# Attention and spectral mixing on one core: how three weight tiles are cut into transfers

## The chip, the core and the metric

The kernel runs on one core of one Trainium2 chip. Its time is the device time of one execution in microseconds (us). The core has five engines that matter here: PE (TensorE, matrix products; its weight loads are listed as PEld), DVE (VectorE), ACT (ScalarE), POOL (GpSimd) and SP (SyncE). Besides these it has 16 DMA engines that move data between the chip's main memory and the core's on-chip memory. To keep the two kinds apart, this text calls a DMA engine a **lane**.

## The reference, cut to what matters

```
attention over 8 batches, 8 heads, 576 positions, 64 per head:
  heads 0-3 see the last 32 positions, heads 4-7 every 32nd position before them
x = attention output as (8, 576, 512)
X = rfft(x, axis=1)[:, :64]                       # 64 modes, real part Xr, imaginary part Xi
Yr = Xr @ w_r - Xi @ w_i                          # one 512x512 matrix of each kind per mode
Yi = Xr @ w_i + Xi @ w_r
u = x + irfft(Y)                                  # Y is zero beyond the 64 modes
out = u + relu(u @ w_ch)
```

The two weight arrays moe_w_r and moe_w_i have shape (64, 512, 512) in 32-bit floats, 64 MB each. Every element is used once per execution, for all 8 batches.

## The kernel before, in words

The program works in stages. First come the four strided heads of the 8 batches, then the four local heads, with the Fourier transform of each finished batch into 64 modes (`dft`). Beside the local heads and after them, PE multiplies the spectra by the weights mode by mode (`mode`, `mode_pair`, L585 to L647). Then w_ch is applied, the spectra are brought back to positions, and the output is written at the end, by SP.

**Weights.** The input dimension is cut into two halves of 256 rows. A weight tile `wt` (L164 and L166) holds one half of two neighbouring modes, in 16-bit floats: 128 partitions of 2 modes x 4 x 512 elements. Partitions 0 to 63 hold the real part, from moe_w_r, and partitions 64 to 127 the imaginary part, from moe_w_i. One partition, called a **row** below, is 8 KB in the tile (two pieces of 4 KB, one per mode) and 16 KB in main memory, since the transfer also turns 32-bit into 16-bit floats. There are 64 tiles. `w_fetch` (L157) makes one tile's transfers; the list `ORDER` (L150) says which half and modes are next, and the index `i` counts modes, so tiles have even `i`.

**Transfers.** POOL issues all loads of weights and of q, k and v, on one queue. A tile normally takes two transfers of 512 KB: the 64 real rows (L186, moe_w_r) and then the 64 imaginary rows (L186, moe_w_i). The last two tiles, and mode 0's imaginary part, are loaded one mode at a time (L190). The dictionary `UNEVEN` (L152) names three tiles whose real part is cut by rows into pieces, each a transfer of its own (L182): tile i = 64 into 25, 12 and 27 rows, tile 80 into 6, 54 and 4, tile 96 into 10 and 54.

**What sets the order.** Nothing is scheduled automatically: instructions run on each engine in the order of the program text. `w_fetch` is called after the products that use up a tile (L608, L638), because the new tile takes that tile's buffer; there are 5 buffers in the pool, and three more tiles lie in space that is used for something else later (`GUEST`). POOL's transfers use 8 semaphores in turn, so a transfer is issued only after the one eight places before it has landed in full, that is, on all its lanes. PE's products on a tile wait for both of its parts. The last products are those of L630, after which come a short chain through `spec_z` (L741), ACT, and the output loop (L1063 to L1088).

Of the kernel before, what the change touches and what calls it, by code (L numbers as in the profile page):

```python
# [56 lines left out]
def kernel(  # L57
# [91 lines left out]
    SPLIT1, SPLIT0 = 56, 48  # L149
    ORDER = [(1, m) for m in range(SPLIT1)] + [(0, m) for m in range(SPLIT0)]  # L150
    ORDER += [(1, m) for m in range(SPLIT1, NM)] + [(0, m) for m in range(SPLIT0, NM)]
    UNEVEN = {64: (25, 12, 27), 80: (6, 54, 4), 96: (10, 54)}  # L152
    w_tiles = []
    w_chs = {}
    w_ch = big.tile([128, 4, DM], F16, name="w_ch")
# [1 line left out]
    def w_fetch(n=1):  # L157
        for _ in range(n):
# [9 lines left out]
            for ri, src in enumerate((moe_w_r, moe_w_i)):  # L168
# [8 lines left out]
                if ri and not m:  # L177
                    ones = [1]
                elif i in UNEVEN and not ri:
                    a = 0  # L180
                    for n in UNEVEN[i]:
                        nc.gpsimd.dma_start(dst[a : a + n], rows[a : a + n])  # L182
# [937 lines left out]
```

## Time and profile before

| what | us |
|---|---|
| runs | 426.20, 426.51, 426.53 |
| their median | 426.51 |
| the profiled execution | 426.5 |
| its span, first to last instruction | 424.7 |
| PE busy | 341.0 |
| DVE busy | 234.6 |
| ACT busy | 218.9 |
| POOL busy | 110.7 |
| issue of the three tiles' first pieces | 218.32, 256.30, 296.81 |
| landing of the last weight transfer | 391.40 |

The span is that of the instructions; 1.8 us of the execution lie around it. A POOL entry in the trace is the issue of a transfer, some 0.6 us, and not the transfer itself, which lands some 18 us later. The share of the DMA engines in a view is their mean busy share; since a packet of 4 KB is recorded with 324 ns while the next one on its lane starts 304.5 ns after it, a lane that is never idle is shown as 1.06.

### The profile page before, as it was taken

How to read it: one execution, taken by the hardware profiler on the slowest of the kernel's cores; microseconds unless marked ns; L12 is line 12 of the kernel's file. 1: busy time of each engine (PE TensorE's matmuls, PEld its weight loads, DVE VectorE, ACT ScalarE, POOL GpSimd, SP SyncE). 2: the span in 40 equal slices, each digit the busy share in tenths (PEclk: the TensorE clock that was granted, in tenths of full speed). 3: DMA queues.
4: the chain of work that ended last, by engine and by line, in shares of the span. 5: the costliest groups of instructions: out<-in, count | busy, mean ns of one | idle time of the engine just before them, and what ended most of it. 6: DMA issues, size and time to landing. Idle time of an engine off the chain costs nothing.

```text
span 424.7 us, 9761 instructions
## 1 busy us (share of the span) xinstructions
PE 341.0 (80%) x4167; PEld 205.9 (48%) x4167; DVE 234.6 (55%) x466; ACT 218.9 (52%) x391; POOL 110.7 (26%) x196
## 2 busy tenths in 40 slices
PE   2977878769999698889758589778788866988994
PEld 2866766654656365566423344435345422544331
DVE  3788778851455154356113346845676363664785
ACT  1687778643656366656642334423443443543773
POOL 7332333322422222222222322222232221220000
PEclk9999999967999699999995989999999968999998
DMA  8999999999999999999999999999999999996598
GB/s 147 212 213 213 213 211 213 211 212 211 213 215 213 211 215 213 214 213 215 210 214 212 214 212 215 211 213 214 213 213 213 214 213 215 213 213 137 205 357 329
DMA packets 30842, 91.62 MB, mean 216 GB/s; under 512 B 4368, under 2 KB 5136, under 8 KB 30800
## 3 DMA queue, kind: packets, MB, share of 16 engines
q0 software_dynamic: 25168, 81.28, 96.6%
q1 hardware_dynamic: 5200, 9.65, 6.2%
q8 instruction: 32, 0.52, 0.5%
q10 hardware_dynamic: 432, 0.08, 0.1%
q14 instruction: 10, 0.08, 0.0%
HBM read 162.83 MB, written 9.44 MB: 406 GB/s over the span
## 4 chain that ended last, share of the span: by engine, by line
DMA 52%; PE 25%; DVE 12%; ACT 4%; issue 3%; POOL 1%; DVEq 0%; POOLq 0%; ACTq 0%
DMA wt<-in_moe_w_i_dram 36%; DMA wt<-in_moe_w_r_dram 12%; PE y L597 5%; DMA ring<-in_q_dram 3%; DVE xb L241 3%; DVE kz L283 2%; ACT X L251 2%; PE p L993 2%; PE sc L532 1%; PE p L1007 1%; PE tp L413 1%; PE y L532 1%; DVE yy L757 1%; DMA ring<-in_v_dram 1%; PE sc L459 1%
## 5 line engine op out<-in xcount | busy, mean ns | idle before, releaser
L597 PE MATMUL y<-wt,X 128*32 128x512 f16 (+1 forms) x448 | 68.1, 415 | 22.7 <-DMA wt<-in_moe_w_i_dram 22.2
L186 POOL DMA_DIRECT2D wt<-in_moe_w_r_dram x59 | 34.6, 587 | 118.5 <-PE y L597 28.2
L186 POOL DMA_DIRECT2D wt<-in_moe_w_i_dram x60 | 35.4, 589 | 75.3 <-DMA wt<-in_moe_w_i_dram 52.9
L597 PEld LDWEIGHTS <-X 128*32 128x32 f16 (+1 forms) x448 | 27.9, 139 | 40.3 <-DMA wt<-in_moe_w_i_dram 20.2
L731 ACT ACTIVATE v<-sc 128x512 f16<-128x512 f32 x32 | 19.1, 597 | 44.5 <-PE sc L722 44.5
L732 DVE COPY xo<-tp 128x512 f16<-128x512 f16 x32 | 22.1, 691 | 35.4 <-PE tp L730 35.4
L722 PE MATMUL sc<-w_cp,xT 128*128 128x512 f16 x128 | 36.1, 404 | 1.9 <-DVE xT L690 1.9
L241 DVE TENSOR_TENSOR xb<-av,rec 90x256 f16<-90x256 f32 (+2 forms) x80 | 36.0, 450 | 2.8
L489 ACT ACTIVATE PL<-sc 128x480 f16<-128x480 f32 (+1 forms) x48 | 26.9, 578 | 20.3 <-PE sc L475 19.9
L240 DVE RECIPROCAL rec<-av 90x4 f32<-90x4 f32 (+2 forms) x80 | 14.6, 182 | 38.1 <-PE av L504 28.2
L251 ACT ACTIVATE yr<-y 128x512 f16<-128x512 f32 x28 | 16.7, 597 | 35.8 <-PE y L597 35.7
L967 DVE TENSOR_TENSOR xo<-p,xo 128x1024 f16<-128x1024 f32 x16 | 19.6, 1224 | 20.8 <-PE p L765 20.7
L420 DVE COPY qT<-tp 128x576 f16<-128x576 f16 x16 | 11.9, 752 | 34.1 <-PE tp L413 34.1
L251 ACT ACTIVATE v<-p 128x1024 f16<-128x1024 f32 x16 | 16.4, 1024 | 22.4 <-PE p L765 22.4
L378 ACT ACTIVATE PL<-sc 90x360 f16<-90x360 f32 (+1 forms) x48 | 22.7, 490 | 7.1 <-PE sc L371 6.5
L251 ACT ACTIVATE v<-tp 128x640 f16<-128x640 f16 (+1 forms) x24 | 19.0, 806 | 11.5 <-PE tp L447 9.3
L413 PE MATMUL tp<-cI_s,ring 64*64 64x64 f16 x864 | 22.2, 195 | 2.8 <-DVE qT L420 2.4
L459 PE MATMUL sc<-cMl_s,cI_s 128*128 128x480 f16 (+1 forms) x48 | 19.0, 395 | 4.8 <-ACT PL L489 3.2
L276 PE MATMUL tp<-cI_s,ring 72*128 72x72 f16 x256 | 15.4, 207 | 9.1 <-DMA ring<-in_v_dram 7.7
L251 ACT ACTIVATE kz<-tp 64x360 f16<-64x360 f16 (+1 forms) x32 | 18.9, 592 | 6.1 <-PE tp L413 5.1
L413 PEld LDWEIGHTS <-ring 64*64 64x64 f16 x864 | 17.3, 109 | 9.1 <-issue 5.1
L1030 ACT ACTIVATE rl<-p 128x1024 f32<-128x1024 f32 (+1 forms) x19 | 18.4, 979 | 5.7 <-PE p L1007 3.0
(142 smaller groups left out, 734.7 us busy)
## 6 DMA issues: line engine op xcount, KB each, us to landing
wt<-in_moe_w_i_dram POOLq DMA_DIRECT2D x60, 512.0 KB, 18.9
wt<-in_moe_w_r_dram POOLq DMA_DIRECT2D x59, 512.0 KB, 18.0
out_dram<-osb SPq DMA_DIRECT2D x17, 512.0 KB, 3.3
ring<-in_v_dram POOLq DMA_DIRECT2D x8, 288.0 KB, 13.2
ring<-in_q_dram POOLq DMA_DIRECT2D x8, 288.0 KB, 13.4
ring<-in_k_dram POOLq DMA_DIRECT2D x8, 288.0 KB, 13.0
ring<-in_v_dram POOLq DMA_DIRECT2D x3, 512.0 KB, 14.9
ring<-in_q_dram POOLq DMA_DIRECT2D x3, 512.0 KB, 14.8
```

The costliest lines, as they stand in the source:

```text
L186: nc.gpsimd.dma_start(dst, rows)
L241: nc.vector.tensor_tensor(out=dst, in0=val.rearrange("p h (q c) -> p h c q", c=4), in1=rec[0:n, 0:pieces] .to_broadcast((n, pieces, 64)) . ...
L251: nc.scalar.activation(out=out, in_=in_, func=ACTF.Copy)
L378: nc.scalar.activation(out=PS[0:n, ds(POFF[t], 4 * n)], in_=scp[0:n, 0 : 4 * n], func=ACTF.Exp, scale=SCALE,)
L413: nc.tensor.transpose(tp[ds(64 * hp, 64), ds(64 * i, 64)], qn[ds(64 * hp, 64), ds(64 * (9 * g + i), 64)], idn[ds(64 * hp, 64), ds(64 * hp, ...
L459: nc.tensor.matmul(scp[:, 0 : n * times].rearrange("p (h x) -> p h x", h=times), idn, mask_rows("cMl", n, times), start=True, stop=False,)
L489: nc.scalar.activation(out=dst, in_=src, func=ACTF.Exp, scale=SCALE)
L597: nc.tensor.matmul(yp[ds(a, 32), :], Xh[half][pr, c].rearrange("p b r (h m) -> p (b r h) m", h=2)[:, :, mm % 32], wt[pr, XC[c], :], start= ...
L722: nc.tensor.matmul(vp, xT[:, ch], w_chs["cp"][:, ch, :], start=(ch == 0), stop=(ch == 3),)
L731: nc.scalar.activation(out=v0, in_=vp, func=ACTF.Copy)
L732: nc.vector.tensor_copy(out=xo.rearrange("p (h q c) -> p h q c", h=2, c=4), in_=tp[:, 0:512].rearrange("p (h c q) -> p h q c", h=2, c=4),)
L967: nc.vector.tensor_tensor(out=xo, in0=up[:, 0:n], in1=xo, op=AluOp.add)
```

## The change

The dictionary `UNEVEN` keeps one entry with other numbers. The real part of tile 64 comes as 16, 35 and 13 rows, and the real parts of tiles 80 and 96 are each loaded as one transfer of 64 rows by L186, as those of the other tiles are. All else is the same.

```diff
-    UNEVEN = {64: (25, 12, 27), 80: (6, 54, 4), 96: (10, 54)}
+    UNEVEN = {64: (16, 35, 13)}
```

## The prediction

> **What bounds the kernel now.** I read the page's slices first, then the stretches of the span, then the chain of waits.
>
> ```profile
> DMA  8999999999999999999999999999999999996598
> GB/s 147 212 213 213 213 211 213 211 212 211 213 215 213 211 215 213 214 213 215 210 214 212 214 212 215 211 213 214 213 213 213 214 213 215 213 213 137 205 357 329
> q0 software_dynamic: 25168, 81.28, 96.6%
> DMA 52%; PE 25%; DVE 12%; ACT 4%; issue 3%; POOL 1%; DVEq 0%; POOLq 0%; ACTq 0%
> ```
>
> From slice 2 to slice 36 the lanes are full, at 211 to 215 GB/s, and one queue (q0, POOL's loads) does it. How the loads end is in the stretches (the columns are us, POOL busy, granted clock, DMA share, GB/s):
>
> ```profile
> 385.00:386.00 1.00, 0.00 (x0) 1.00 1.01 205
> 386.00:387.00 1.00, 0.00 (x0) 1.00 0.98 193
> 387.00:388.00 1.00, 0.00 (x0) 1.00 0.95 188
> 388.00:389.00 1.00, 0.00 (x0) 1.00 0.79 156
> 389.00:390.00 1.00, 0.00 (x0) 1.00 0.52 102
> 390.00:391.00 1.00, 0.00 (x0) 1.00 0.17 33
> ```
>
> A full lane shows 1.06. The share falls over 6 us, so the 16 lanes finish the same queue at very different times. The lane time missing from 385 on is (0.05 + 0.08 + 0.11 + 0.27 + 0.54 + 0.89)/1.06 = 1.8 us per lane: an even split of the same bytes would end 1.8 us sooner. And the last lane is what the end waits for (chain of waits: start, us, what):
>
> ```profile
> 381.41 9.99 DMA wt<-in_moe_w_i_dram
> 391.40 0.14 issue
> 391.54 0.65 PE y L630 x16
> ```
>
> PE had stood idle 0.52 us there for that transfer. What comes after, up to 424.7, needs those products, so **the end moves one for one with the lane that finishes last**. The change moves rows between lanes; that is its whole price, and I work it out lane by lane.
>
> **Lanes from packets.** The trace keeps start, length and size of every packet. On one lane a 4 KB packet is followed after 304.5 ns, and each transfer ends with a 4-byte receipt that takes 20.7 ns. By these two steps the packets sort into 16 lanes. A whole part puts 4 rows on each (8 packets, 2.46 us). The pieces do not spread like that:
>
> ```profile
> wt<-in_moe_w_r_dram POOLq DMA_DIRECT2D x2, 432.0 KB, 17.0
> ...
> wt<-in_moe_w_r_dram POOLq DMA_DIRECT2D x1, 216.0 KB, 14.4
> wt<-in_moe_w_r_dram POOLq DMA_DIRECT2D x1, 200.0 KB, 16.1
> ```
>
> The 54 rows (432 KB) lie on 9 lanes, 6 rows each; the 27 on 9, 3 each; the 25 on 5, 5 each; 12, 10, 6 and 4 rows on as many lanes, one each. In each case that is the largest divisor of the rows up to 16. A lane without a share gets, for two packets of a row, two 4-byte fillers instead. The count closes: under 512 B the page has 4368 packets, and 213 transfers x 16 receipts + 384 of constants + 576 fillers is 4368. On the first tile one lane has (5, 1, 0) rows of the three pieces, four have (5, 0, 3), five (0, 1, 3), six (0, 1, 0): each piece begins on the lane after the one where the last piece stopped, round a ring of 16. I number the places 0 to 15 from the first lane of the 25 rows. All three tiles fit that ring. In rows over the three real parts (12 is even), with the time of the lane's last receipt:
>
> | places | rows now | last receipt, us |
> |---|---|---|
> | 0 | 13 | 387.0 |
> | 1 to 4 | 15 | 388.3 to 389.9 |
> | 5, 6 | 11 | 390.4, 390.6 |
> | 7, 8 | 16 | 388.9, 389.5 |
> | 9 | 11 | 391.1 |
> | 10 to 12 | 9 | 388.5, 389.9, 390.4 |
> | 13 to 15 | 9 | 385.2, 389.5, 390.7 |
>
> Why lanes differ is seen too: the 32 instruction loads (q8, 16 KB) take 0.9 to 1.15 us each and fall on about half of the lanes; the last, at 385.66, made place 9 the last one.
>
> **The change, part by part.**
>
> *Pieces 16, 35, 13.* By the divisor, 16 rows take 16 lanes, 35 take 7 lanes with 5 rows, 13 take 13 lanes with one. From place 0 that is 7 rows on places 0 to 3, 6 on 4 to 6, 2 on 7 to 15.
>
> *Tiles 80 and 96 whole.* 4 rows on each lane, twice, so 8 more everywhere.
>
> *Sum in rows, new less old:* place 0: 15 - 13 = +2; 1 to 3: 0; 4: -1; 5 and 6: 14 - 11 = **+3**; 7 and 8: -6; 9: -1; 10 to 15: +1. They add to zero. One row is 2 x 304.5 ns = 0.61 us. New ends: places 5 and 6 at 390.4 and 390.6 + 1.83 = 392.2 and 392.4; 13 to 15 at most 390.7 + 0.61 = 391.3; 10 to 12 at most 391.0; 9 at 390.5; all others earlier. Off that comes what is in the lanes besides rows: three receipts fewer (0.06) and, on places 5 and 6, some 20 fillers of 6 to 8 ns (0.14). The last receipt goes from 391.1 to about 392.2: **+1.1 us**.
>
> *Three issues fewer on POOL.* Its order of time around the first tile (start, us, what, idle before):
>
> ```profile
> 218.32 0.70 POOL L182 DMA_DIRECT2D wt<-in_moe_w_r_dram  x1 [2.19 <-DMA wt<-in_moe_w_r_dram]
> 219.17 0.57 POOL L182 DMA_DIRECT2D wt<-in_moe_w_r_dram  x1 [0.16 <-issue]
> 221.63 0.62 POOL L182 DMA_DIRECT2D wt<-in_moe_w_r_dram  x1 [1.88 <-DMA wt<-in_moe_w_r_dram]
> ```
>
> Issues of 0.57 to 0.70 us cost nothing either way: POOL waits about 2 us for a landing before nearly each of them, and a transfer issued 18 us ahead of its landing leaves several in each lane. Were that cover gone, three issues are 2 us. All later transfers take another of the 8 semaphores; each still waits for the one eight before, and this holds more bytes when none of the eight is a piece. No wait is added, and nothing is queued behind one.
>
> *The middle.* Lanes lie up to 9.0 us apart after tile 80 now, and would lie some 7 us apart. Weights would land sooner there, but PE waits only 5.4 us in all for weights from 256 to 313, and the lanes stay full, so nothing of it reaches the end.
>
> *Where the ring begins.* The trace can't show whether an execution starts where the last one stopped. Before's pieces advance it by 64 and its twelve 8-row loads by 96, both multiples of 16, so either way each execution looks alike. The new pieces advance it by 7 + 13 = 20, so it would move on 4 places each time. With the start 4 on, places 4 to 7 take +3 and 8 to 10 +2 against even loads, 9 ends at 392.9: +1.9. Starts 8 and 12 on load the late places 9 to 15: +2.7 and +3.1 by the same sums. I take 1.5, between the profiled start (1.1) and one move (1.9), and keep 1.1 and 3.1 for the range.
>
> **Two rules weighed.** The trace has the 54 rows on 9 lanes and the fillers on 7. The Trainium skill (DMA: Bandwidth & Descriptors, Why a DMA increments its semaphore by 16 and not by 1) states that divisor rule and a round-robin start, but also an exception where such copies go out as rows/16 rounded up per engine; by the exception 35 rows would be 3 on eleven lanes and 2 on a twelfth, and the early lanes alone would be loaded. The trace shows the divisor, not the exception. The same page (Anatomy of one DMA — SWDGE (gpsimd) path) gives each transfer a fixed 2.0 us; as an estimate from it, three fewer would give back 6 us, to about 420. The trace has 0.02 us for a receipt in a full lane, since transfers queue back to back.
>
> **The forecast.** Profiled execution: 424.7 + 1.5 = 426.2 in span, + 1.8 around it = 428.0. Its 426.5 is the median of the runs (426.51), so 428.0 stands for the median too.
>
> **The rivals.**
>
> *No change that can be measured (within 0.2%, about what a measurement here can tell from no change; 425.66 to 427.36).* The instruction loads decide as much as rows: place 5 or 6 took one of 1.05 us at 360.1, the other a smaller one of 0.45 at 343.6. If these fall on other lanes, 5 and 6 end 0.5 to 1 us sooner, the last lane is near 391.3, and the time is 426.7 to 427.2. Against it: they come in the same turn of lanes all through the trace, and the change alters no engine's program but by three issues.
>
> *Faster.* Loading whole ends the crowding of tile 80: its last piece lands 4.2 us after the part before it, where a whole part takes 2.45. If PE, falling behind there, carried that delay to the end, 1.7 us would come back: 424.8. It decides if lanes run dry because buffers come free late. Against it: the share is 1.06 to 1.07 in every stretch from 218 to 382, and there is no lane time to win but the tail. With rows, even the best start can't gain: all whole would end with place 13 to 15 at 390.7 + 1.83 = 392.5.
>
> *Ring moved far (starts 8 and 12):* 429.2 to 429.6, if the start carries over and these executions set the median.
>
> **How the numbers follow.** Slower at the profiled start or one move on, 427.4 to 428.5: 0.54, of which 428.0 is the middle. Moved far: 0.16. Same: 0.20. Faster: 0.10. Range 426.7 to 429.4: it leaves out the faster case and a little at each end. Chances: faster 0.10, same 0.20, slower 0.70.
>
> **What would show it.** The last weight transfer lands near 392.5 to 393.3 instead of 391.40. From 256 to 313 lanes lie nearer together than now, and in the last 6 us further apart, with the share falling for longer. The fillers fall from 384 in the pieces to 9 x 10 + 3 x 2 = 96, and the packets under 512 B from 4368 to 4032 (three times 16 receipts go too); that many says 35 rows lie on 7 lanes and 13 on 13. Runs that differ by steps of about a microsecond would show the ring carried over. A landing at or before 391.40 would prove the sum wrong, a share under 1.0 before 382 the premise.

## The result and the profile after

The changed kernel takes 427.8 us (median of 9 runs, 426.92 to 428.25), the kernel before beside it 426.64 us (9 runs, 426.0 to 427.42). The medians differ by 1.2 us. The ratio is 1.0024, with a 95% interval from 1.0014 to 1.0033, which is a loss of 1.0 us (0.6 to 1.4): small, but clear of no change. A second set of runs (f1 below) gave 428.22 us and 1.0031 [1.0019, 1.0044].

The page of the profiled execution (428.25 us, span 426.5 us):

```profile
DMA packets 30507, 91.62 MB, mean 215 GB/s; under 512 B 4033, under 2 KB 4801, under 8 KB 30465
...
q0 software_dynamic: 24832, 81.28, 96.3%
```

Queue q0 moves the same 81.28 MB in fewer packets. Packets under 512 B are 4033, where the prediction had 4032: q14, a queue of instruction loads, has one packet of 64 bytes more here, and the repeat (f1) has 4032. So the pieces lie as the divisor rule said: 16 rows on 16 lanes, 35 on 7, 13 on 13.

The chain of waits at the end (start, us, what):

```profile
363.52 17.22 DMA wt<-in_moe_w_r_dram
...
383.49 9.60 DMA wt<-in_moe_w_i_dram
393.08 0.14 issue
393.22 0.65 PE y L630 x16
```

It is the chain of before, 1.7 us later: the last weight transfer lands at 393.08 instead of 391.40, and PE starts 0.14 us after it in both. The stretches before that end (us, POOL busy, granted clock of TensorE, DMA share, GB/s):

```profile
386.00:387.00 1.00, 0.00 (x0) 1.00 0.99 197
387.00:388.00 1.00, 0.00 (x0) 1.00 0.88 180
388.00:389.00 1.00, 0.00 (x0) 1.00 0.73 143
389.00:390.00 1.00, 0.00 (x0) 1.00 0.71 139
390.00:391.00 1.00, 0.00 (x0) 1.00 0.40 78
391.00:392.00 1.00, 0.00 (x0) 1.00 0.09 16
392.00:393.00 1.00, 0.00 (x0) 1.00 0.04 8
```

One lane of 16 at 1.06 would show 0.066. From 391.71 on, where the second-latest lane has landed its last packet, the core waits 1.4 us for a single lane, while the other 15 are idle. Traced back by its packets, this lane took five rows of the 35 and one row of the 16 and none of the 13: it is place 5 or 6.

### The profile page after: what moved, and what is told of

It is laid out like the page before. It is cut to its first block, busy times and chain, and to the rows that moved or that the text cites. A ratio compares the mean times of both kernels' runs of the same rounds, so it can differ in the third digit from the quotient of the medians.

```text
span 426.5 us, 9756 instructions
## 1 busy us (share of the span) xinstructions
PE 342.9 (80%) x4167; PEld 206.0 (48%) x4167; DVE 234.8 (55%) x466; ACT 219.1 (51%) x391; POOL 107.9 (25%) x193
## 2 busy tenths in 40 slices
DMA packets 30507, 91.62 MB, mean 215 GB/s; under 512 B 4033, under 2 KB 4801, under 8 KB 30465
## 3 DMA queue, kind: packets, MB, share of 16 engines
q0 software_dynamic: 24832, 81.28, 96.3%
## 4 chain that ended last, share of the span: by engine, by line
DMA 58%; PE 22%; DVE 10%; ACT 4%; issue 3%; POOL 1%; DVEq 0%; POOLq 0%; ACTq 0%
DMA wt<-in_moe_w_i_dram 41%; DMA wt<-in_moe_w_r_dram 12%; DMA ring<-in_q_dram 5%; PE y L597 4%; DVE xb L241 2%; DVE kz L283 2%; ACT X L251 2%; PE p L993 2%; PE sc L532 1%; PE p L1007 1%; PE tp L413 1%; PE sc L459 1%; PE y L532 1%; DVE kz L420 1%; DVE rec L240 1%
## 5 line engine op out<-in xcount | busy, mean ns | idle before, releaser
L597 PE MATMUL y<-wt,X 128*32 128x512 f16 (+1 forms) x448 | 69.1, 421 | 24.1 <-DMA wt<-in_moe_w_i_dram 23.6
L186 POOL DMA_DIRECT2D wt<-in_moe_w_r_dram x61 | 35.5, 582 | 127.8 <-DMA wt<-in_moe_w_r_dram 31.5
L186 POOL DMA_DIRECT2D wt<-in_moe_w_i_dram x60 | 35.0, 583 | 79.7 <-DMA wt<-in_moe_w_i_dram 65.1
```

The costliest lines, as they stand in the source:

```text
L186: nc.gpsimd.dma_start(dst, rows)
L597: nc.tensor.matmul(yp[ds(a, 32), :], Xh[half][pr, c].rearrange("p b r (h m) -> p (b r h) m", h=2)[:, :, mm % 32], wt[pr, XC[c], :], start= ...
```

## The experiments

There are twelve runs. All their kernels differ from the changed one in the dictionary `UNEVEN` at most: f1 is the changed kernel itself, g3 repeats e1, and none leaves out any work. A last landing is always that of the profiled execution. **Theory:** rows decide, lane by lane; the end follows the lane that finishes last, and a piece costs nothing by itself. **Rivals:** pieces cost something as transfers (issues, receipts, semaphores); or the instruction loads decide, by the lane on which they fall.

### All whole (e1, and g3 as its repeat)

```diff
-    UNEVEN = {64: (16, 35, 13)}
+    UNEVEN = {}
```

> All three real parts loaded whole, no pieces at all. Lane theory (the end is the lane that finishes last, at 0.61 us a row): places 10 to 12 get 3 rows more than before and end at 390.4 + 1.83 = 392.2, place 9 one more at 391.7, places 5 and 6 one more at 391.2; the last lane ends 1.1 us later than before, so the time is 1.1 us above before, 0.6 to 1.7 with the instruction loads falling on other lanes. Piece theory (a piece costs time of its own, whole parts save it): at or below the time of before, -0.3 us. Instruction-load theory (only where the 16 KB instruction loads fall matters, rows do not): same as before within 0.5 us.

> All three tiles whole once more, beside the two others. As before: 426.9, at most 0.4 us above the kernel before; between the early pieces (g1) and the changed kernel. Lane theory: last landing 391.6 to 392.1 by which late lane the last instruction loads fall on.

Measured: 426.86 us, ratio to before 1.0005 [0.9996, 1.0014]; the repeat 426.98 us, 1.0006 [0.9997, 1.0015]. So before's eight pieces were worth some 0.2 us (0.6 at most by the intervals), not 1.1, and the expectation of e1 missed. By themselves these two runs would fit the rival of the instruction loads, which had the same time as before within 0.5 us; e3, e4 and f3 below decide against it. The chain of e1:

```profile
382.46 9.63 DMA wt<-in_moe_w_i_dram
392.09 0.14 issue
392.22 0.65 PE y L630 x16
```

The last landing is 0.7 us behind before's in this execution and 1.0 us ahead of the changed kernel's. With even loads the landings also show which lanes are late by themselves. The last transfer lands on its 16 lanes (receipts that the trace records, us) at

```
386.35 386.53 386.85 387.07 387.42 387.59 387.90 388.79
390.45 391.04 391.09 391.42 391.44 391.70 391.82 392.09
```

These are two groups of eight, some 4 us apart in the mean, and between them half of the lanes work, at a share of 8 x 0.066 = 0.53:

```profile
388.00:389.00 1.00, 0.00 (x0) 1.00 0.56 111
389.00:390.00 1.00, 0.00 (x0) 1.00 0.51 102
```

By the prediction's table, less the rows that each place had, places 0 to 4, 7, 8 and 15 are the early lanes, 5, 6 and 9 to 14 the late ones. The instruction loads make the gap. When e1's packets from 256 us on are sorted into lanes, the eight loads of 16 KB lie on the eight late lanes, one on each, and each delays its lane by 1.08 to 1.13 us. Before that end 31 such loads fall on eight lanes, 3.9 on each, which is 4.2 to 4.4 us.

### Half of the change (e2, e3)

```diff
-    UNEVEN = {64: (16, 35, 13)}
+    UNEVEN = {64: (25, 12, 27)}                                        # e2
+    UNEVEN = {64: (16, 35, 13), 80: (6, 54, 4), 96: (10, 54)}          # e3
```

> Half of the change alone: tile 64 keeps 25, 12 and 27 rows, tiles 80 and 96 are whole. Lane theory: places 10 to 15 stay relieved by 3 rows on tile 64 as before, place 9 gets one row more (391.7), places 5 and 6 one more (391.2); last lane 0.6 us later than before, time +0.6 us (0.1 to 1.1). Piece theory: five pieces fewer, between before and below it, 0 to -0.5 us. Instruction-load theory: same within 0.5 us.

> The other half alone: tile 64 in 16, 35 and 13 rows, tiles 80 and 96 in their old pieces. The ring then stands at 4 instead of 10 when tile 80 comes, so the same old pieces lie on other lanes: rows against whole are +2, +7, +7, +2, +2, +2, +2 on places 0 to 6, -2 on 7 to 9, -3 on 10 to 15. Lane theory: places 5 and 6 end at 392.3 to 392.4, places 1 and 2 somewhere from 390.7 to 393.1; time +1.3 us on before (0.9 to 2.0), as slow as the whole change or slower although it has eight pieces as before. Piece theory: as before, within 0.3 us. Instruction-load theory: same within 0.5 us.

Measured: e2 426.82 us, 1.0006 [0.9997, 1.0015]; e3 427.92 us, 1.003 [1.0019, 1.0042]. Loading tiles 80 and 96 whole costs nothing that shows. The numbers 16, 35 and 13 alone bring the whole loss: with five more pieces (three more transfers) e3 is as slow as the changed kernel, though the old pieces of tiles 80 and 96 lie on other lanes there than before.

### The same pieces on other places (e4)

```diff
-    UNEVEN = {64: (16, 35, 13)}
+    UNEVEN = {62: (8, 56), 64: (16, 35, 13)}
```

> The changed kernel with one tile more in pieces: tile 62 comes as 8 and 56 rows, which is nearly even by itself (one row more on places 0 to 5, three fewer on 6 and 7) but moves the ring by 22, so that the 16, 35 and 13 rows of tile 64 begin at place 6 and lie on the late lanes 8 to 12. Lane theory: places 8 and 9 get +3 and 10 to 12 +2 against whole, 9 ends at 393.5 and 10 to 12 at 393.4, 2.3 us later than before; time +2.3 us (1.7 to 2.9), 1.2 us slower than the changed kernel. Piece theory: two pieces more cost a little, +0.1 us on the changed kernel. Instruction-load theory: as the changed kernel within 0.5 us.

Measured: 428.67 us, 1.0051 [1.0038, 1.0064], last landing 393.50. Tile 62's pieces only move the start of the ring by six and are almost even by themselves; with them the late places 9 to 12 get 2 or 3 rows more than even loads have, and some 0.9 us more is lost than by the changed kernel.

### The changed kernel again (f1)

> The changed kernel once more, beside the others. Lane theory, ring starting at place 0 in each execution: places 5 and 6, which are late already, get 2 rows more than in even loads, and the last of them ends near 392.4 to 393.1; 427.2 to 428.3 us, above whole loads by some 1 us. If the start of the ring were carried over from one execution to the next, the profiled one would have an even chance or better of another start: the seven lanes of the 35 rows would not be five early and two late ones, and the runs would lie in steps, up to 429.6. If only the turn of the instruction loads decides, as likely 426.6 as 428.

Measured: 428.22 us (427.61 to 429.07), 1.0031. The profiled execution ends at 392.48, and its pieces show the same start of the ring. The six runs show no steps of a microsecond.

### One set of pieces in two orders (f2, f3)

```diff
-    UNEVEN = {64: (16, 35, 13)}
+    UNEVEN = {64: (15, 25, 24), 80: (25, 24, 15)}      # f2
+    UNEVEN = {64: (24, 25, 15), 80: (24, 25, 15)}      # f3
```

> Lane theory: tiles 64 and 80 in pieces that give places 0 to 4 and 15, the early lanes, 5, 4, 4, 4, 1 and 2 rows more than even loads, and all others, the late ones among them, 2 rows less. The late lanes end 1.2 us sooner than with whole loads, the early ones come up to about 390.0; last landing 390.3 to 391.0, time 425.3 to 426.1, below before by 0.5 to 1.3 us. Rival, that pieces cost in themselves (six pieces here against three in the changed kernel): 428 or above. Rival, that the turn of the instruction loads decides: 426.6 to 427.9.

> The same six sizes in the same two tiles in another order (24, 25, 15 twice). Lane theory: now places 12 to 15 get 4 rows more than even loads, place 0 gets 6, all others 2 less; places 12 to 14 are late lanes and end near 393.7 to 394.5: time 428.8 to 429.7, above before by 2.2 to 3.1 us, and 3 us or more above the other order. Rivals, pieces in themselves or the turn of the instruction loads: the two orders agree within 0.6 us.

Measured: f2 426.85 us, 1.0001 [0.9993, 1.001]; f3 429.63 us, 1.0066 [1.0054, 1.0079]. Six pieces of the same sizes, 2.8 us apart by their order: this is the clearest case against both rivals, that pieces cost something and that the instruction loads decide, for by either the two orders agree. The stretches of f3:

```profile
390.00:391.00 1.00, 0.00 (x0) 1.00 0.21 41
391.00:392.00 1.00, 0.00 (x0) 1.00 0.27 57
392.00:393.00 1.00, 0.00 (x0) 1.00 0.16 33
393.00:394.00 1.00, 0.00 (x0) 1.00 0.10 20
394.00:395.00 1.00, 0.00 (x0) 1.00 0.02 4
```

From 391 on the share is that of three lanes, then two, then one (3 x 0.066 = 0.20, the first stretch with an instruction load at 391.3 besides): the last landings are 392.95, 394.12 and 394.66, by the ring the three late lanes 12 to 14, which got 4 rows more.

f2 missed its number by some 1 us. Its late lanes did land sooner, 390.95 at the latest by the receipts; but one lane of places 0 to 3 landed at 391.70. It carries 4 or 5 rows more than even loads, so by rows it would land at 391.70 - 4 x 0.61 = 389.3 with even loads (388.7 with 5), near the latest of e1's early group (388.79) and not with the rest of it. A load of 8 KB (q14) falls on it at 343.2 and costs it 0.5 us. The estimate had all early lanes alike.

### Fewer rows for all late lanes (f4, g1, g2, h1)

```diff
-    UNEVEN = {64: (16, 35, 13)}
+    UNEVEN = {64: (18, 21, 25), 72: (10, 50, 4), 80: (21, 3, 40), 96: (27, 30, 7)}   # f4
+    UNEVEN = {64: (25, 24, 15)}                                                      # g1
+    UNEVEN = {64: (25, 24, 15), 72: (7, 56, 1), 80: (9, 50, 5), 96: (24, 13, 27)}    # g2
+    UNEVEN = {64: (25, 11, 28), 72: (18, 40, 6), 80: (8, 50, 6), 96: (26, 11, 27)}   # h1
```

> Lane theory: four tiles (64, 72, 80 and 96) in twelve pieces that take 2 to 4 rows from each late lane (places 5, 6 and 9 to 14) and give places 0 to 4 and 15 two to five more, 7 and 8 one: all lanes but 7, 8 and 15 would end between 389.0 and 390.3. Last landing 389.8 to 390.6, time 424.9 to 425.7, below before by 0.9 to 1.7 us. An even split of all lanes, which nothing beats, would be 1.8 us below. Rival, pieces cost in themselves: the slowest of the four. Rival, turn of the instruction loads: 426.6 to 427.9.

> Three pieces on tile 64 only, as in the changed kernel, but 25, 24 and 15 rows: against whole loads place 0 gets 3 rows more, 1 to 4 get 2 more, 5 to 15 one less. Lane theory: the late lanes (5, 6, 9 to 14) end 0.6 us sooner than with whole loads, places 1 to 4 end at 390.0 at most; last landing 390.9 to 391.6, time 426.0 to 426.7, which is 1.5 to 2.2 us below the changed kernel with as many pieces. Rival, three pieces on that tile cost in themselves: like the changed kernel, near 428.2.

> Four tiles in twelve pieces, as in the run with four tiles before, but one lane among places 1 to 3, which that run showed to end 1.4 us later than was taken for it, gets less: places 0 to 4 get 4, 3, 3, 3 and 3 rows more than whole loads, 7, 8 and 15 get 2 more, 5, 6 and 10 to 13 three less, 9 and 14 two less. Lane theory: late lanes end 1.2 to 1.8 us sooner than with whole loads, the lane among 1 to 3 at 390.6; last landing 390.4 to 391.0, time 425.5 to 426.1, below before by 0.5 to 1.2 us. Rival, pieces in themselves, or whatever kept the last run with four tiles at 427.1, keep it there: 427.

> Four tiles in twelve pieces again, without a piece of a single row and with only 2 rows more than whole loads on places 1 to 4, 7, 8 and 15 (place 0 gets 5 more); 5, 6, 9, 10 and 11 get 2 less, 12 to 14 three less. Lane theory, with the one-row piece on two lanes as the cause of 428.7 in the last run with four tiles: late lanes end at 390.8 at the latest, the lane among 1 to 3 at 390.0; last landing 390.4 to 391.1, time 425.5 to 426.3, below before by 0.4 to 1.2 us, the fastest of all. Rival, twelve pieces cost something in themselves or the turn of the instruction loads undoes it: 427 or above.

Measured:

| kernel | last landing | us | ratio to before |
|---|---|---|---|
| f4 | 391.66 | 427.09 | 1.0008 [0.9996, 1.002] |
| g1 | 391.30 | 426.69 | 0.9995 [0.9984, 1.0006] |
| g2 | 393.79 | 428.69 | 1.0037 [1.0023, 1.0051] |
| h1 | 390.58 | 426.24 | 0.9996 [0.9986, 1.0006] |

*f4* missed its 424.9 to 425.7 us as f2 had missed. It again loads places 1 to 3 by 4 rows, and again a single lane is last, 0.7 us behind the next.

*g1* has three pieces on tile 64, like the changed kernel, and ends at 391.30 instead of 393.08 or 392.48. It is what the theory gives for early lanes loaded instead of late ones, and the rival would have put it at 428.2.

*g2* was to be fast and was slow; its count of packets says why, as far as is known:

```profile
DMA packets 30842, 91.62 MB, mean 214 GB/s; under 512 B 4368, under 2 KB 5136, under 8 KB 30800
```

216 transfers of 16 receipts, 384 of constants, 192 fillers of the 8-row loads and 322 of the eleven larger pieces leave 4368 - 4354 = 14 for the piece of one row. If its two packets lay on one lane, 15 lanes would have two fillers each, 30. Fourteen says that the two packets lie on two lanes and 14 lanes have one filler. The ring then moves by 2 and not by 1, and all later pieces lie one place further than planned: place 9, a late one, gets 2 rows more than even loads instead of 2 less, and ends at 393 or later. That the last lane is place 9 is worked out, not seen. By the same count place 0 gets 7 rows more, but it is an early lane, and with 6 more in f3 it is not among the last three as read above. Nor do 2 rows explain all of it: the other kernels with 2 rows more end at 392.5 to 393.1, and g2 ends at 393.79. That part stays open.

*h1*, without such a piece, has the lanes nearest together of all kernels (387.74 to 390.58, against 385.50 to 391.40 before). Its stretches:

```profile
387.00:388.00 1.00, 0.00 (x0) 1.00 0.95 188
388.00:389.00 1.00, 0.00 (x0) 1.00 0.74 148
389.00:390.00 1.00, 0.00 (x0) 1.00 0.34 66
390.00:391.00 1.00, 0.00 (x0) 1.00 0.00 0
```

The profiled execution, 425.69 us, is the shortest of all, and twelve pieces cost nothing that shows. But its runs go from 425.69 to 427.16 us, and against before's the median is only 0.24 us lower, with 1 inside the interval. Of the 0.8 us that its profiled end gains on before's, the runs show at most a part: it can't be said to beat the kernel before.

### What the twelve say together

Rows of the worst late place, counted against even loads (places after the ring), and the end of the profiled execution:

| rows | kernel | last landing |
|---|---|---|
| -2 | h1 | 390.58 |
| -1 | g1; before | 391.30; 391.40 |
| 0 | e1, g3; e2 | 392.09, 391.99; 391.47 |
| +2 | after, f1; e3 | 393.08, 392.48; 392.65 |
| +2 (worked out) | g2 | 393.79 |
| +3 | e4 | 393.50 |
| +4 | f3 | 394.66 |

From -2 to +4 the end moves by 4.08 us, 0.68 a row, where a row is 0.61; kernels of one line differ by up to 0.6 (g2 by more). The runs rise less steeply: by the ratios, from 0.2 us below before (h1) to 2.8 above (f3), 0.5 a row. f2 and f4 (-2) are left out, since an early lane ends last there.

## Why the prediction came out right, step by step

- **The end follows the last lane: shown.** The profiled time less the last landing is 35.10 us before, 35.17 after, and 35.11 to 35.14 in ten of the twelve others, over landings from 390.58 to 394.66. The two exceptions are g2 (35.53) and e2 (35.98). In e2 the transfer landed at 391.47, but the chain is another (g2's is of the same kind):

```profile
390.71 0.64 PE y L630 x16
391.35 0.86 PE p L993 x4
392.21 0.43 PE p L998 x2
392.64 0.49 PE y L630 x16
```

  PE had just begun other products (L993, L998) that stand ahead of the last ones in its program, and finishes them first. So this order is the next bound: the last products begin 1.2 us after the landing in this case, where 0.14 us is the rule.

- **The divisor and the ring: right.** The count of packets and the lanes of the 35 rows agree. The rule gives the count under 512 B of the other kernels too (4224 for f2 and f3, 4416 for h1; g2 by the one-row piece as above), and e4 and f3 use it to put a loss where it is wanted. The exception that the Trainium skill states (DMA: Bandwidth & Descriptors, Why a DMA increments its semaphore by 16 and not by 1), rows over 16 rounded up, would give other fillers and load twelve lanes with the 35 rows, so not the early lanes alone as the prediction has it; 4032 is the divisor's number.

- **Three rows more on places 5 and 6: right lane, right size.** The last receipt was to come at 392.2 to 392.4; it came at 392.73 in the first profiled execution and at 392.13 in f1. The packets of this lane show a load of 16 KB at 277.6 us in the first, with a loss of 1.08 us, and one at 318.5 in f1. That the turn of these loads makes the difference of 0.6 is argued, not shown.

- **The step that was mis-sized: what the old pieces were worth.** The prediction had even loads ending at 392.5 on places 13 to 15, later than the change. e1 and g3 measure 426.86 and 426.98 us, 0.2 to 0.3 us above before by the ratios, and end at 392.09 and 391.99. Two entries of the table were at fault: where two lanes run in step in before's trace, their packets had been read crosswise, and the latest of places 13 to 15 is 389.5 and not 390.7 (the 390.6 or so belongs to one of places 1 to 4). The load of 8 KB at 343.6, which the rival gave to place 5 or 6, lies on that early lane as well. So the loss is not the going of the old pieces; it is the new ones, some 0.8 to 1.1 us (the ratios of the changed kernel and f1 less those of e1 and g3).

- **The ring moved on between executions: not seen.** I took 1.5 us between 1.1 (profiled start) and 1.9 (four places on). The profiled executions of the changed kernel both begin at place 0, and the runs lie in no steps. Without this term the sum of 1.1 stands, and the ratios measure 1.0 and 1.3 us: the lane sum was right, and the 0.4 us added for the ring was not. That 428.0 lies so near 427.8 and 428.2 is in part luck, since the kernel before, too, was 0.1 to 0.3 us slower beside them than the 426.51 the forecast started from. The start in executions without a profile is not shown by any trace.

- **Three issues fewer, nothing: right.** e3, with three transfers more than the changed kernel, is 0.1 us from it, and h1, with twelve pieces and six transfers more, is the lowest of all. The fixed 2.0 us for each transfer that the same page states (Anatomy of one DMA — SWDGE (gpsimd) path) is not to be seen in a queue that stays full.

- **The middle, nothing: right.** Lanes lie 6.9 us apart from 277 on, against up to 9.0 before; PE's waits for weights from 256 to 313 go from 5.4 to 5.0 us, and the end shows nothing of it.

- **The rival "no change", by the instruction loads: part of it stands.** Kernels with the same rows differ by 0.6 us in their profiled ends (393.08 and 392.48), and single runs of one kernel mostly by 1 to 2 us. The turn of the 32 loads begins on different lanes in different profiled executions. That this makes the spread of the runs is argued from the traces; no run varied it alone.

## What to carry to other kernels

Before loads are balanced by hand over DMA engines, look at the landings of one transfer on all 16: the engines that are late, and by how much, decide what an uneven cut is worth, and here a row on the wrong lane costs 0.5 to 0.7 us at the end, while the same row on an early lane is free as long as that lane stays ahead of the late ones (with 4 rows more, in f2 and f4, one did not). Work out for every piece on how many engines it falls and where the next one begins, since in g2, where by the count of packets the ring was off by one place, 1.6 us was lost. When the cut brings less than the spread that other traffic makes (0.6 us here), load whole: that was 0.2 to 0.3 us from before's eight pieces (with no difference inside the interval), and it is simpler.

## What the runs showed of the hardware that was not expected

Instruction loads of 16 KB fall on only eight of the 16 DMA engines, in turn; in e1 each costs its engine 1.08 to 1.13 us of a full queue, and after 31 of them those eight are some 4 us late. A piece of one row, two packets of 4 KB, goes to two engines and moves the start of the next transfer by two, by the count of fillers (14, not 30). Six more transfers with their receipts and fillers (h1 against the changed kernel) cost nothing that the runs show.
